# Evicting the queries of two attention branches one 512-wide unit at a time, branch by branch, where pairs of both branches were evicted together

## The chip, the cores and the metric

The kernel runs on one core of a Trainium2 chip. The metric is the device time of one execution in microseconds; the profile is one execution recorded by the hardware profiler, whose span runs from the first to the last instruction.

## The reference

Two linear-attention branches, A and B, read the same input x (2048 rows of 640) and are mixed by a gate. Each has its own weights. 32 heads of width 20; everything is bf16 outside the kernel.

```python
def branch(x, wqkv, wo):
    q, k, v = split_heads(x @ wqkv)                  # 32 heads of 20
    phi = lambda t: where(t > 0, t + 1, exp(t)) + 1e-6
    pq, pk = phi(q), phi(k)
    kv  = einsum("bhsd,bhse->bhde", pk, v)
    z   = sum_s(pk)
    num = einsum("bhqd,bhde->bhqe", pq, kv)
    den = einsum("bhqd,bhd->bhq", pq, z) + 1e-6
    return merge_heads(num / den) @ wo

g = sigmoid((x * gate_w).sum(-1))
out = g * branch(x, A...) + (1 - g) * branch(x, B...)
```

## The kernel before

The kernel never forms the values. It runs these stages:

1. **Keys** (`k_part`, `k_both`): per tile of 128 rows, x @ wk for A and B, and phi of it into `PK`. phi is three instructions: an exp on ScalarE from PSUM into the buffer `EK` (L560), a min-and-add on VectorE within `EK` (L564), and a max-and-add on VectorE from PSUM and `EK` into the result (L570). For most tiles a unit is 128 x 512.
2. **G** (`g_unit`): phi(k) transposed times x, five parts per branch, 16 tiles deep. Each is copied out and transposed by a DMA into `GT`. `gone["A"]` and `gone["B"]` name the last matmul of each branch's G.
3. **M** (`m_unit`): GT times wv gives the 32 small kv matrices, which VectorE masks (L651) into `MB`. **Weight products** (`wp_unit`): M times wo, six tiles per branch, copied to `WS`, stored to memory by `wp_store` (tensor `wrowsB` for B) and read back in another order by `wp_rows` into `WP` (WPA, WPB). So phi(q) @ WP is already num @ wo.
4. **Queries** (`q_pair`): the rows are cut into four blocks b of 512, the 640 columns into five parts k. One call does one (b, k) for both branches: ten matmuls of 512 columns, five for A into one PSUM bank and five for B into the bank beside it, then phi over 128 x 1024 at once (exp L753, min-and-add L755, max-and-add L759) into `FE`, whose halves `PQ` are the phi(q) of A and B. `FE` is shared with `PK`, so the queries may only begin when G has read the keys.
5. **Denominators** (`dens`) for two blocks at a time: phi(q) times `ZBD`, copied with the epsilon added into `DN` (L791). **Scaling** (`scale_q`) per block: reciprocal into `RC` (L802), a store of it to memory (`factor`), a load that spreads it over the partitions (`RX`), and multiplies in place over phi(q) of A and B (L820).
6. **Finals** (`final`): per tile of 128 rows, phi(q) @ WPA and phi(q) @ WPB, each two groups of 320 columns in a pair of banks; ScalarE scales A by its gate (L865), VectorE scales B and adds (L871), and SP stores the row tile.

All matmuls of a tile go through one helper, so they all carry L383; tell them by tile names: `ps<-XT,WQA` and `ps<-XT,WQB` are queries, `ps<-FE,ZBDA` and `ps<-FE,ZBDB` denominators, `ps<-WPA,FE` and `ps<-WPB,FE` finals. DMAs carry L372.

**Order.** Nothing runs in the order written by itself. Every operation is put into a planner (`_Sched`) with a duration from simple formulas and a latency of 180 or 190 ns to its readers. The planner simulates the engines: at each step it takes, for the engine that can start earliest, among the operations that could start within 20 ns of the earliest the one that was written first. So a call that is written earlier ranks higher. PSUM's eight banks and the rings of buffers (`EK`: six slots of 640, used by the queries before as three double slots) are given out in the same simulation. The result is a fixed order per engine; on the chip each engine runs its list in that order and waits by semaphores. A late operand therefore holds everything behind it on that engine.

The order in which the second half is written, before the change: block 0 of the queries, M of B, block 1, denominators of blocks 0 and 1, block 2, scaling of 0, block 3, scaling of 1, denominators of blocks 2 and 3, finals of block 0, scaling of 2, finals of 1, scaling of 3, finals of 2 and 3. The weight products of B are placed between the pairs of block 1 by `WPAT`, the last of them after the first pair of block 2, followed there by the store and the load of its rows.

Of the kernel before, what the change touches and what calls it, by code (L numbers as in the profile page):

```python
# [15 lines left out]
ACT = mybir.ActivationFunctionType  # L16
ALU = mybir.AluOpType

S = 2048
D = 640  # L20
# [4 lines left out]
NC = 5  # L25
EPS = 1e-6
HALF = 320
WPAT = ((1, 0), (1, 1), (1, 2), (1, 3), (1, 4), (2, 0))
XW = 672
PE_GHZ = 2.4  # L30

# [255 lines left out]
def _act_ns(n, psum=True):  # L287
    return n / 1.2 + (52.0 if psum else 94.0)


def _dve_ns(n, rate=1):
    return n / (0.96 * rate) + 68.0
# [6 lines left out]
def bass_gated_mix__linear_attn_block__linear_attn_block__prompt_kernel(nc, A_x, A_wqkv, A_wo, B_x, B_wqkv, B_wo, gate_w, out):  # L299
# [4 lines left out]
    XS = ("A", "B")  # L304

    with ExitStack() as es:
# [6 lines left out]
        XT = sb("XT", [128, NC, S])  # L313
        WQ = {X: sb("WQ" + X, [128, NC, D]) for X in XS}
# [4 lines left out]
        FE = sb("FE", [128, 2, NT * D])  # L319
        PKJ = FE[:, :, :].rearrange("p x (t f) -> p x t f", f=D)  # L320
        PK = {X: PKJ[:, x, :, :] for x, X in enumerate(XS)}
        PQ = {X: FE[:, x, :].rearrange("p (k s) -> p k s", s=S) for x, X in enumerate(XS)}
# [9 lines left out]
        NEK = 6  # L332
        EK = sb("EK", [128, NEK, D])
# [25 lines left out]
        def pair(t, n):  # L359
            b0, b1 = t.banks  # L360
            return PS[:, b0 : b1 + 1, 0:n]
# [15 lines left out]
        def mms(name, steps, reads, writes, cols, lat=190.0, par=1, prio=None, after=None):  # L377


            def fn(pe):  # L380
                ins = None
                for o, l, r, a, z, tp in steps():
                    ins = pe.matmul(o, l, r, start=a, stop=z, tile_position=tp, skip_group_check=True)  # L383
                return ins

            return sch.op("PE", fn, cols / PE_GHZ / par, reads=reads, writes=writes, name=name, lat=lat, prio=prio, after=after)
# [93 lines left out]
                    _dve_ns(128 * (c1 - c0)), reads=[(tt,)], writes=[("XTC", t, c) for c in range(c0, c1)], name="xev%d" % t,  # L480
                )

        ring = {"ek": _Ring(NEK), "eq": _Ring(NEK // 2), "dn": _Ring(2), "rx": _Ring(2), "os": _Ring(NOS), "ts": _Ring(NTS)}

        def phi_k(X, t, tile):
            es = _Tile(1, ring["ek"])
# [203 lines left out]
        def wp_store(X):  # L690
            dma(
                "SP", "ws" + X, WD[X].ap()[0:600, :].rearrange("(q p) f -> p q f", p=120), WS[:, 0:5, :], reads=[("WS", q) for q in range(5)],
                writes=[("WD", X, 0)], us=2.0,
            )
# [32 lines left out]
                "DVE", lambda e: e.reciprocal(GA[:, :, :], GE[:, :, :]), 330, reads=[("GE", 0), ("GE", 1)], writes=[("GA",)], name="ga",  # L727
            )

        def q_pair(b, k):  # L730

            tile = _Tile(2)
            es = _Tile(1, ring["eq"])

            def eq():
                return EK[:, :, :].rearrange("p n f -> p (n f)")[:, 1280 * es.slot : 1280 * es.slot + 1024]

            def eq2():
                return eq().rearrange("p (x s) -> p x s", x=2)

            dst = FE[:, :, S * k + 512 * b : S * k + 512 * b + 512]
            span = range(S * k + 512 * b, S * k + 512 * b + 512)
            over = [("F", X, w, t) for X in XS for w in ("k", "k5") for t in range(span[0] // D, span[-1] // D + 1)]

            def steps():
                return [
                    (PS[:, tile.banks[x], :], WQ[X][:, c, k : D : NC], XT[:, c, 512 * b : 512 * b + 512], c == 0, c == NC - 1, None)
                    for x, X in enumerate(XS) for c in range(NC)
                ]

            xt = [("XTC", t, c) for t in range(4 * b, 2) for c in range(NC)] + [("XT", t) for t in range(max(2, 4 * b), 4 * b + 4)]
            o = mms("q%d%d" % (b, k), steps, xt + [("WQ", X) for X in XS], [(tile,)], 2 * NC * 518, after=gone["B"])
            sch.op("ACT", lambda e: e.activation(eq2(), pair(tile, 512), ACT.Exp), _act_ns(1024), reads=[(tile,)], writes=[(es,)], name="eq%d%d" % (b, k))  # L753
            sch.op(
                "DVE", lambda e: e.tensor_scalar(eq(), eq(), 1.0, EPS, op0=ALU.min, op1=ALU.add), _dve_ns(1024, 4),  # L755
                reads=[(es,)], writes=[(es,)], name="tq%d%d" % (b, k),
            )
            sch.op(
                "DVE", lambda e: e.scalar_tensor_tensor(out=dst, in0=pair(tile, 512), scalar=0.0, in1=eq2(), op0=ALU.max, op1=ALU.add),  # L759
                _dve_ns(1024), reads=[(tile,), (es,)], writes=[("PQ", X, k, b) for X in XS] + over, name="sq%d%d" % (b, k),  # L760
            )
            return o

        def dens(b0):

            dtile = _Tile(1)

            def den():
                r = []
                for k in range(NC):  # L770
                    for x, X in enumerate(XS):
                        q = PQ[X][:, k, 512 * b0 : 512 * b0 + 1024].rearrange("p (b h f) -> p b h f", b=2, h=2)
                        for h in (0, 1):
                            g = 2 * x + h
                            r.append((
                                PS[32 * g : 32 * g + 32, dtile.banks[0], :].rearrange("p (b f) -> p b f", b=2), ZBD[X][:, k, :],
                                q[:, :, h, :], k == 0, k == NC - 1, (0, 32 * g),
                            ))
                return r

            mms(
                "den%d" % b0, den, [("ZBD", X) for X in XS] + [("PQ", X, k, b) for X in XS for k in range(NC) for b in (b0, b0 + 1)],
                [(dtile,)], 5 * 540,
            )
            ds = []
            for b in (b0, b0 + 1):
                d = _Tile(1, ring["dn"])
                ds.append(d)
                sch.op(
                    "ACT",  # L790
                    lambda e, d=d, lo=256 * (b - b0): e.activation(  # L791
                        DN[:, d.slot, :], PS[:, dtile.banks[0], lo : lo + 256], ACT.Identity, bias=EP[:, 0:1]
                    ),
                    _act_ns(256), reads=[(dtile,), ("EP",)], writes=[(d,)], name="dn%d" % b,
                )
            return ds

        def scale_q(b, ds, pieces):

            def rec(e):  # L800
                with nc.allow_low_precision(reason="the factor is a bf16 matmul operand"):
                    return e.reciprocal(RC[:, ds.slot, :], DN[:, ds.slot, :])  # L802

            sch.op("DVE", rec, 1740, reads=[(ds,)], writes=[(ds,)], name="rc%d" % b)
            rep = FD[b].ap()
            dma(
                "SP", "fw%d" % b, rep.rearrange("g h r f -> (g h) r f"), lambda: RC[:, ds.slot, :].unsqueeze(1).to_broadcast([128, 4, 256]),
                reads=[(ds,)], writes=[("FD", b)], us=0.6,
            )
            xs = _Tile(1, ring["rx"])  # L810
            dma(
                "SP", "fr%d" % b, lambda: RX[:, xs.slot, :].rearrange("p (g f) -> p g f", f=256), rep.rearrange("g h r f -> (h r) g f"),
                reads=[("FD", b)], writes=[(xs,)], us=0.6,
            )
            w = 512 // pieces
            for j in range(pieces):
                for x, X in enumerate(XS):
                    def fn(e, j=j, x=x, X=X):
                        v = PQ[X][:, :, 512 * b + w * j : 512 * b + w * j + w]
                        return e.tensor_tensor(  # L820
                            out=v, in0=v, in1=RX[:, xs.slot, 512 * x + w * j : 512 * x + w * j + w].unsqueeze(1).to_broadcast([128, NC, w]), op=ALU.mult
                        )
                    ts = range(4 * b + 4 * j // pieces, 4 * b + 4 * (j + 1) // pieces)
                    sch.op(
                        "DVE", fn, _dve_ns(NC * w, 2), reads=[(xs,)] + [("PQ", X, k, b) for k in range(NC)],
                        writes=[("PQS", X, t) for t in ts], name="ml%s%d" % (X, b),
                    )
# [98 lines left out]
        wp_store("A")  # L926
        zbd("B")
        def queries(b):
            for k in range(NC):
                q_pair(b, k)  # L930
                for i, p in enumerate(WPAT):
                    if p == (b, k):
                        wp_unit("B", (i - 1) % 6)
                        if i == 0:
                            wp_rows("A")
                        if i == 5:
                            wp_store("B")
                            wp_rows("B")

        def finals(b):  # L940
            for t in range(4 * b, 4 * b + 4):
# [5 lines left out]
        queries(0)  # L947
        m_unit("B")
        queries(1)
        d0, d1 = dens(0)  # L950
        queries(2)
        scale_q(0, d0, 2)
        queries(3)
        scale_q(1, d1, 2)
        d2, d3 = dens(2)
        finals(0)
        scale_q(2, d2, 2)
        finals(1)
        scale_q(3, d3, 4)
        finals(2)  # L960
        finals(3)

# [32 lines left out]
```

## Time and profile before

| | us |
|---|---|
| median of 3 runs | 192.31 (191.86 to 192.77) |
| profiled execution | 191.86 |
| its span | 190.5 |
| TensorE / VectorE / ScalarE busy in it | 185.6 / 125.7 / 73.0 |
| query stage on TensorE (first query to the last) | 94.96 to 143.3 |
| second denominator | from 148.95 |

TensorE is PE in the profile, VectorE DVE, ScalarE ACT, SyncE SP, whose queue issues most DMAs. Lines of the timelines give start, duration, engine, line, operation, result<-operands with shapes, a count where neighbours are merged, and in brackets the idle time of the engine before it with what ended that. Lines of the groups give busy time in all, mean ns of one instruction, and idle time before the group with what ended it. A line of the windows gives the stretch, its length, the busy time of PE, PEld (weight loads), DVE, ACT and POOL with their counts, the granted TensorE clock, the DMA share and GB/s. The granted clock was 1.00 in every stretch of the profile.

### The profile page before, as it was taken

How to read it: one execution, taken by the hardware profiler on the slowest of the kernel's cores; microseconds unless marked ns; L12 is line 12 of the kernel's file. 1: busy time of each engine (PE TensorE's matmuls, PEld its weight loads, DVE VectorE, ACT ScalarE, POOL GpSimd, SP SyncE). 2: the span in 40 equal slices, each digit the busy share in tenths (PEclk: the TensorE clock that was granted, in tenths of full speed). 3: DMA queues.
4: the chain of work that ended last, by engine and by line, in shares of the span. 5: the costliest groups of instructions: out<-in, count | busy, mean ns of one | idle time of the engine just before them, and what ended most of it. 6: DMA issues, size and time to landing. Idle time of an engine off the chain costs nothing.

```text
span 190.5 us, 3131 instructions
## 1 busy us (share of the span) xinstructions
PE 185.6 (97%) x1280; PEld 124.2 (65%) x1289; DVE 125.7 (66%) x235; ACT 73.0 (38%) x109; POOL 8.2 (4%) x14
## 2 busy tenths in 40 slices
PE   7999999999999999999999999999979999999995
PEld 2655555555888888888855655555536577777774
DVE  0399898989500019996157896679699977943324
ACT  2265556555211221113244366654443413331332
POOL 8900000000000000000000000000000000000000
DMA  6999699991011111113152023069400154311212
GB/s 192 286 225 198 194 390 364 342 235 31 0 38 34 34 34 38 34 34 38 34 126 70 3 58 137 9 156 271 121 0 0 69 153 140 107 53 50 72 69 69
DMA packets 31967, 21.48 MB, mean 113 GB/s; under 512 B 16850, under 2 KB 31698, under 8 KB 31954
## 3 DMA queue, kind: packets, MB, share of 16 engines
q1 hardware_dynamic: 31234, 20.48, 39.5%
q10 hardware_dynamic: 720, 0.82, 1.3%
q8 instruction: 10, 0.16, 0.4%
q14 instruction: 3, 0.02, 0.0%
HBM read 12.05 MB, written 5.31 MB: 91 GB/s over the span
## 4 chain that ended last, share of the span: by engine, by line
PE 88%; DMA 6%; DVE 4%; issue 1%; ACT 0%; DVEq 0%
PE ps L383 87%; DMA factor<-RC 3%; DMA XN<-in_A_x_dram 2%; DVE FE L820 2%; DMA RX<-factor 1%; DVE FE L759 1%; DVE RC L802 1%; PE ps L468 1%; DVE EK L755 0%; DVE OL L871 0%; ACT DN L791 0%; DVEq L276 0%
## 5 line engine op out<-in xcount | busy, mean ns | idle before, releaser
L383 PE MATMUL ps<-XN,FE 128*128 128x320 bf16 x320 | 44.3, 300 | 0.0
L383 PE MATMUL ps<-WK,XT 128*128 128x512 bf16 (+2 forms) x246 | 43.7, 337 | 0.2
L383 PEld LDWEIGHTS ps<-XN,FE 128*128 128x128 bf16 x320 | 37.5, 118 | 6.0
L383 PEld LDWEIGHTS ps<-WK,XT 128*128 128x128 bf16 x250 | 24.2, 98 | 19.2 <-issue 0.2
L753 ACT ACTIVATE EK<-ps 128x1024 bf16<-128x1024 f32 x20 | 20.5, 1023 | 24.0 <-PE ps L383 21.9
L560 ACT ACTIVATE EK<-ps 128x512 bf16<-128x512 f32 (+1 forms) x42 | 21.4, 526 | 16.2 <-PE ps L383 16.2
L383 PE MATMUL ps<-XT,WQA 128*128 128x512 bf16 x95 | 24.0, 379 | 1.6 <-DVE FE L759 1.0
L383 PE MATMUL ps<-XT,WQB 128*128 128x512 bf16 x100 | 24.8, 379 | 0.0
L759 DVE SCALAR_TENSOR_TENSOR FE<-ps,EK 128x1024 bf16<-128x1024 f32 x20 | 24.3, 1217 | 0.4
L383 PE MATMUL ps<-WPA,FE 128*128 128x320 bf16 (+1 forms) x165 | 24.5, 295 | 0.0
L383 PE MATMUL ps<-WPB,FE 128*128 128x320 bf16 (+1 forms) x165 | 24.5, 295 | 0.0
L570 DVE SCALAR_TENSOR_TENSOR FE<-ps,EK 128x512 bf16<-128x512 f32 (+1 forms) x42 | 23.9, 597 | 0.5
L865 ACT ACTIVATE TS<-ps,GA 128x640 f32<-128x640 f32 (+2 forms) x18 | 13.1, 734 | 27.5 <-PE ps L383 27.5
L871 DVE SCALAR_TENSOR_TENSOR OS<-ps,GA,TS 128x640 bf16<-128x640 f32 x15 | 13.0, 876 | 13.3 <-PE ps L383 13.3
L597 ACT ACTIVATE GS<-ps 128x640 bf16<-128x640 f32 x10 | 7.0, 703 | 36.8 <-PE ps L383 36.8
L383 PEld LDWEIGHTS ps<-WPA,FE 128*128 128x128 bf16 x165 | 15.9, 98 | 6.5 <-issue 0.4
L383 PEld LDWEIGHTS ps<-WPB,FE 128*128 128x128 bf16 x165 | 15.9, 98 | 5.8
L383 PEld LDWEIGHTS ps<-XT,WQB 128*128 128x128 bf16 x100 | 11.7, 117 | 9.8
L383 PEld LDWEIGHTS ps<-XT,WQA 128*128 128x128 bf16 x100 | 11.5, 118 | 10.0 <-DVE FE L759 1.5
L711 DVE SCALAR_TENSOR_TENSOR GP<-XN,GWB 128x640 bf16<-128x640 bf16 x16 | 13.3, 828 | 4.1 <-PE ps L383 3.6
L820 DVE TENSOR_TENSOR FE<-FE,RX 128x1280 bf16<-128x1280 bf16 (+1 forms) x20 | 12.7, 688 | 3.4 <-DMA RX<-factor 3.4
L564 DVE TENSOR_SCALAR EK<-EK 128x512 bf16<-128x512 bf16 (+1 forms) x42 | 11.3, 271 | 3.0
(52 smaller groups left out, 78.7 us busy)
## 6 DMA issues: line engine op xcount, KB each, us to landing
out_dram<-OS SPq DMA_DIRECT2D x15, 160.0 KB, 1.8
XN<-in_A_x_dram SPq DMA_DIRECT2D x3, 640.0 KB, 8.1
factor<-RC SPq DMA_DIRECT2D x4, 256.0 KB, 3.2
RX<-factor SPq DMA_DIRECT2D x4, 256.0 KB, 3.0
WVA<-in_A_wqkv_dram SPq DMA_DIRECT2D x1, 800.0 KB, 10.6
WQA<-in_A_wqkv_dram SPq DMA_DIRECT2D x1, 800.0 KB, 11.9
WVB<-in_B_wqkv_dram SPq DMA_DIRECT2D x1, 800.0 KB, 11.3
WQB<-in_B_wqkv_dram SPq DMA_DIRECT2D x1, 800.0 KB, 12.1
```

What stands on the lines that cost most here:

```text
L383: ins = pe.matmul(o, l, r, start=a, stop=z, tile_position=tp, skip_group_check=True)
L468: ins = pe.transpose(PSB[:, tt.banks[0], 128 * c : 128 * c + 128], XN[:, t, 128 * c : 128 * c + 128], IDN[:, :])
L560: "ACT", lambda e, ps=ps, ek=ek: e.activation(ek(), ps(), ACT.Exp), _act_ns(n), reads=[(tile,)], writes=[(es,)],
L564: "DVE", lambda e, ek=ek: e.tensor_scalar(ek(), ek(), 1.0, EPS, op0=ALU.min, op1=ALU.add), _dve_ns(n, 4),
L570: return e.scalar_tensor_tensor(out=out, in0=two(ps()), scalar=0.0, in1=two(ek()), op0=ALU.max, op1=ALU.add)
L597: "ACT", lambda e: e.activation(GS[:, k, :].rearrange("p (h f) -> p h f", f=HALF), pair(tile, HALF), ACT.Copy),
L711: lambda e, t=t: e.scalar_tensor_tensor(out=GP[:, :], in0=XN[:, t, 0:D], scalar=1.0, in1=GWB[:, :], op0=ALU.mult, op1=ALU.mult, accum_out= ...
L753: sch.op("ACT", lambda e: e.activation(eq2(), pair(tile, 512), ACT.Exp), _act_ns(1024), reads=[(tile,)], writes=[(es,)], name="eq%d%d" % ( ...
L759: "DVE", lambda e: e.scalar_tensor_tensor(out=dst, in0=pair(tile, 512), scalar=0.0, in1=eq2(), op0=ALU.max, op1=ALU.add),
L820: return e.tensor_tensor(out=v, in0=v, in1=RX[:, xs.slot, 512 * x + w * j : 512 * x + w * j + w].unsqueeze(1).to_broadcast([128, NC, w]), ...
L865: "ACT", lambda e: e.activation(t_ap(), acc(), ACT.Copy, scale=GA[:, 0, t : t + 1]), _act_ns(hi - lo),
L871: lambda e: e.scalar_tensor_tensor(out=o_ap(), in0=acc(), scalar=GA[:, 1, t : t + 1], in1=t_ap(), op0=ALU.mult, op1=ALU.add),
```

## The change

`q_pair` is replaced by `q_unit`, which does one (b, k) of one branch: five matmuls into one bank, and phi over 128 x 512. There are 40 such units where there were 20 pairs. Further:

- a block is written as its five units of A and then its five units of B, where it was five pairs;
- units of A wait for `gone["A"]`, those of B for `gone["B"]`; the pairs waited for `gone["B"]`;
- the exp result lies in a slot of the ring `EK` with its six slots; the ring of three double slots is gone;
- the weight products of B come two units behind in block 1 (`WPLAG`): after A2, A3, A4, B0, B1 and B2, the last tile number 4 after B2; the store and load of B's rows are written after block 1, and the load of A's rows after A2 of block 1;
- `dens` no longer makes the copies into `DN`; each `scale_q` makes its own;
- the scaling of block 0 is written before block 2, not after it.

```diff
-WPAT = ((1, 0), (1, 1), (1, 2), (1, 3), (1, 4), (2, 0))
+WPLAG = 2
...
-        ring = {"ek": _Ring(NEK), "eq": _Ring(NEK // 2), "dn": _Ring(2), "rx": _Ring(2), "os": _Ring(NOS), "ts": _Ring(NTS)}
+        ring = {"ek": _Ring(NEK), "dn": _Ring(2), "rx": _Ring(2), "os": _Ring(NOS), "ts": _Ring(NTS)}
...
-        def q_pair(b, k):
-
-            tile = _Tile(2)
-            es = _Tile(1, ring["eq"])
...
+        def q_unit(X, b, k):
+            tile = _Tile(1)
+            es = _Tile(1, ring["ek"])
+
+            def ek():
+                return EK[:, es.slot, 0:512]
+
+            dst = PQ[X][:, k, 512 * b : 512 * b + 512]
...
             def steps():
                 return [
-                    (PS[:, tile.banks[x], :], WQ[X][:, c, k : D : NC], XT[:, c, 512 * b : 512 * b + 512], c == 0, c == NC - 1, None)
-                    for x, X in enumerate(XS) for c in range(NC)
+                    (PS[:, tile.banks[0], :], WQ[X][:, c, k : D : NC], XT[:, c, 512 * b : 512 * b + 512], c == 0, c == NC - 1, None)
+                    for c in range(NC)
                 ]
...
-            ds = []
-            for b in (b0, b0 + 1):
-                d = _Tile(1, ring["dn"])
-                ds.append(d)
-                sch.op(
-                    "ACT",
-                    lambda e, d=d, lo=256 * (b - b0): e.activation(
-                        DN[:, d.slot, :], PS[:, dtile.banks[0], lo : lo + 256], ACT.Identity, bias=EP[:, 0:1]
-                    ),
-                    _act_ns(256), reads=[(dtile,), ("EP",)], writes=[(d,)], name="dn%d" % b,
-                )
-            return ds
-
-        def scale_q(b, ds, pieces):
+            return dtile
+
+        def scale_q(b, dtile, pieces):
+
+            ds = _Tile(1, ring["dn"])
+            lo = 256 * (b % 2)
+            sch.op(
+                "ACT",
+                lambda e: e.activation(DN[:, ds.slot, :], PS[:, dtile.banks[0], lo : lo + 256], ACT.Identity, bias=EP[:, 0:1]), _act_ns(256),
+                reads=[(dtile,), ("EP",)], writes=[(ds,)], name="dn%d" % b,
+            )
...
         def queries(b):
-            for k in range(NC):
-                q_pair(b, k)
-                for i, p in enumerate(WPAT):
-                    if p == (b, k):
-                        wp_unit("B", (i - 1) % 6)
-                        if i == 0:
+            for X in XS:
+                for k in range(NC):
+                    q_unit(X, b, k)
+                    q = 5 * (X == "B") + k - WPLAG
+                    if b == 1 and 0 <= q < 6:
+                        wp_unit("B", (q - 1) % 6)
+                        if q == 0:
                             wp_rows("A")
-                        if i == 5:
-                            wp_store("B")
-                            wp_rows("B")
...
         queries(1)
-        d0, d1 = dens(0)
+        wp_store("B")
+        wp_rows("B")
+        d01 = dens(0)
+        scale_q(0, d01, 2)
         queries(2)
-        scale_q(0, d0, 2)
         queries(3)
-        scale_q(1, d1, 2)
-        d2, d3 = dens(2)
+        scale_q(1, d01, 2)
+        d23 = dens(2)
         finals(0)
-        scale_q(2, d2, 2)
+        scale_q(2, d23, 2)
         finals(1)
-        scale_q(3, d3, 4)
+        scale_q(3, d23, 4)
```

More of the change, by code (lines that the diff above doesn't have):

```diff
@@ L728, in gates @@
             )
-        def q_pair(b, k):
-            tile = _Tile(2)
-            es = _Tile(1, ring["eq"])
[L735 to L741, printed above, removed]
+        def q_unit(X, b, k):
[4 more added lines that the diff above has]
+            dst = PQ[X][:, k, 512 * b : 512 * b + 512]
@@ L742, in q_pair @@
             span = range(S * k + 512 * b, S * k + 512 * b + 512)
-            over = [("F", X, w, t) for X in XS for w in ("k", "k5") for t in range(span[0] // D, span[-1] // D + 1)]
+            over = [("F", X, w, t) for w in ("k", "k5") for t in range(span[0] // D, span[-1] // D + 1)]
             def steps():
                 return [
-                    (PS[:, tile.banks[x], :], WQ[X][:, c, k : D : NC], XT[:, c, 512 * b : 512 * b + 512], c == 0, c == NC - 1, None)
-                    for x, X in enumerate(XS) for c in range(NC)
-                ]
@@ L751, in q_pair @@
-            xt = [("XTC", t, c) for t in range(4 * b, 2) for c in range(NC)] + [("XT", t) for t in range(max(2, 4 * b), 4 * b + 4)]
-            o = mms("q%d%d" % (b, k), steps, xt + [("WQ", X) for X in XS], [(tile,)], 2 * NC * 518, after=gone["B"])
-            sch.op("ACT", lambda e: e.activation(eq2(), pair(tile, 512), ACT.Exp), _act_ns(1024), reads=[(tile,)], writes=[(es,)], name="eq%d%d" % (b, k))
+                    (PS[:, tile.banks[0], :], WQ[X][:, c, k : D : NC], XT[:, c, 512 * b : 512 * b + 512], c == 0, c == NC - 1, None)
@@ L754, in q_pair @@
+                    for c in range(NC)
+                ]
+            mms("q%s%d%d" % (X, b, k), steps, [("XTC", t, c) for t in range(4 * b, 2) for c in range(NC)] + [("XT", t) for t in range(max(2, 4 * b), 4 * b + 4)] + [("WQ", X)], [(tile,)], NC * 518, after=gone[X])
             sch.op(
-                "DVE", lambda e: e.tensor_scalar(eq(), eq(), 1.0, EPS, op0=ALU.min, op1=ALU.add), _dve_ns(1024, 4),
-                reads=[(es,)], writes=[(es,)], name="tq%d%d" % (b, k),
+                "ACT", lambda e: e.activation(ek(), PS[:, tile.banks[0], :], ACT.Exp), _act_ns(512), reads=[(tile,)],
+                writes=[(es,)], name="eq%s%d%d" % (X, b, k),
@@ L757, in q_pair @@
             )
             sch.op(
-                "DVE", lambda e: e.scalar_tensor_tensor(out=dst, in0=pair(tile, 512), scalar=0.0, in1=eq2(), op0=ALU.max, op1=ALU.add),
-                _dve_ns(1024), reads=[(tile,), (es,)], writes=[("PQ", X, k, b) for X in XS] + over, name="sq%d%d" % (b, k),
-            )
-            return o
+                "DVE", lambda e: e.tensor_scalar(ek(), ek(), 1.0, EPS, op0=ALU.min, op1=ALU.add), _dve_ns(512, 4),
+                reads=[(es,)], writes=[(es,)], name="tq%s%d%d" % (X, b, k),
+            )
@@ L764, in dens @@
+            sch.op(
+                "DVE",
+                lambda e: e.scalar_tensor_tensor(
+                    out=dst, in0=PS[:, tile.banks[0], :], scalar=0.0, in1=ek(), op0=ALU.max, op1=ALU.add
+                ),
+                _dve_ns(512), reads=[(tile,), (es,)], writes=[("PQ", X, k, b)] + over, name="sq%s%d%d" % (X, b, k),
+            )
         def dens(b0):
@@ L784, in dens @@
             )
-            ds = []
-            for b in (b0, b0 + 1):
-                d = _Tile(1, ring["dn"])
-                ds.append(d)
-                sch.op(
-                    "ACT",
-                    lambda e, d=d, lo=256 * (b - b0): e.activation(
-                        DN[:, d.slot, :], PS[:, dtile.banks[0], lo : lo + 256], ACT.Identity, bias=EP[:, 0:1]
-                    ),
-                    _act_ns(256), reads=[(dtile,), ("EP",)], writes=[(d,)], name="dn%d" % b,
-                )
-            return ds
-        def scale_q(b, ds, pieces):
+            return dtile
+        def scale_q(b, dtile, pieces):
+            ds = _Tile(1, ring["dn"])
+            lo = 256 * (b % 2)
+            sch.op(
+                "ACT",
+                lambda e: e.activation(DN[:, ds.slot, :], PS[:, dtile.banks[0], lo : lo + 256], ACT.Identity, bias=EP[:, 0:1]), _act_ns(256),
+                reads=[(dtile,), ("EP",)], writes=[(ds,)], name="dn%d" % b,
+            )
             def rec(e):
```

## The prediction

> **What bounds the kernel now.** I read the page first, then the groups kept apart by shape, then the timelines around the one place where TensorE stands still, and last the chain of waits.
>
> ```profile
> span 190.5 us, 3131 instructions
> PE 185.6 (97%) x1280; PEld 124.2 (65%) x1289; DVE 125.7 (66%) x235; ACT 73.0 (38%) x109; POOL 8.2 (4%) x14
> PE   7999999999999999999999999999979999999995
> DVE  0399898989500019996157896679699977943324
> PE 88%; DMA 6%; DVE 4%; issue 1%; ACT 0%; DVEq 0%
> ```
>
> TensorE is the bound: 185.6 of 190.5 us. The whole budget for a gain is the 4.9 us in which it is idle, and most of that is the start and the tail, which the change does not touch. The one lower digit inside (7, the 30th slice, 138 to 143 us) lies in the query stage. The timelines of VectorE, TensorE and the SP queue show it:
>
> ```profile
> 133.34 1.23 DVE L759 SCALAR_TENSOR_TENSOR FE<-ps,EK 128x1024 bf16<-128x1024 f32 x1
> 136.22 3.04 DVE L820 TENSOR_TENSOR FE<-FE,RX 128x1280 bf16<-128x1280 bf16 x4 [1.66 <-DMA RX<-factor]
> 139.17 0.76 DVE L755 TENSOR_SCALAR EK<-EK 128x1024 bf16<-128x1024 bf16 x2
> 141.12 1.27 PE L383 MATMUL ps<-XT,WQA 128*128 128x512 bf16 x5 [1.05 <-DVE FE L759]
> 148.95 0.39 PE L383 MATMUL ps<-FE,ZBDA 128*32 128x512 bf16 x2
> 122.89 0.34 SPq L372 DMA_DIRECT2D wrowsB<-WS  x1
> 127.88 0.35 SPq L372 DMA_DIRECT2D WPB<-wrowsB  x1
> 128.28 2.57 SPq L372 DMA_DIRECT2D factor<-RC  x2
> 133.42 1.12 SPq L372 DMA_DIRECT2D RX<-factor  x2
> ```
>
> VectorE waits 1.66 us for the factors of query block 0, multiplies for 3 us, and the query pairs behind it keep their PSUM banks so long that the last pair of block 3 starts 1.05 us late. The factors were late because their store stood in the SP queue behind WPB (issued 127.88, factor 128.28, though the reciprocal ended at 127.15) and shared the DMA engines with its 800 KB: 5.1 us to land, against a median of 3.2. From 148.95 on TensorE never waits again until the tail.
>
> The prices, by shape:
>
> ```profile
> L759 DVE SCALAR_TENSOR_TENSOR FE<-ps,EK 128x1024 bf16<-128x1024 f32 x20 | 24.3, 1217 | 0.4
> L753 ACT ACTIVATE EK<-ps 128x1024 bf16<-128x1024 f32 x20 | 20.5, 1023 | 24.0 <-PE ps L383 21.9 <-DVE FE L759 2.1
> L755 DVE TENSOR_SCALAR EK<-EK 128x1024 bf16<-128x1024 bf16 x20 | 8.4, 424 | 7.2 <-ACT EK L753 7.2
> L570 DVE SCALAR_TENSOR_TENSOR FE<-ps,EK 128x512 bf16<-128x512 f32 x28 | 19.3, 688 | 0.5
> L560 ACT ACTIVATE EK<-ps 128x512 bf16<-128x512 f32 x28 | 16.7, 597 | 16.2 <-PE ps L383 16.2
> L564 DVE TENSOR_SCALAR EK<-EK 128x512 bf16<-128x512 bf16 x28 | 8.2, 294 | 2.4
> ```
>
> The key stage already runs the three instructions of the changed kernel in their exact shapes, so nothing has to be guessed from afar. Its timeline shows how they follow one another, and the windows how full VectorE already is at the end of the query stage:
>
> ```profile
> 30.15 0.56 DVE L564 TENSOR_SCALAR EK<-EK 128x512 bf16<-128x512 bf16 x2
> 30.62 1.02 DVE L570 SCALAR_TENSOR_TENSOR FE<-ps,EK 128x512 bf16<-128x512 f32 x2
> 140.00:150.00 10.00, 8.91 (x71) 5.52 (x70) 10.00 (x13) 3.63 (x4) 0.00 (x0) 1.00 0.01 2
> ```
>
> **Part by part. TensorE.** The same 200 query matmuls, 216 ns each (five start 1.08 us after the five before). Reordering them costs nothing: weights change at every matmul in both forms.
>
> **Splitting the evictions.** Two halves for one whole: 2 x 688 - 1217 = 159 ns and 2 x 294 - 424 = 164 ns on VectorE, 2 x 597 - 1023 = 171 ns on ScalarE. Times 20: 6.5 us more VectorE work (125.7 to 132.2), 3.4 us more on ScalarE. ScalarE has 1.08 us for a unit of 0.60, plus 0.70 for each of six weight tiles that TensorE also spends 0.27 us on; it stays hidden (uncovered, 3.4 us). VectorE needs 0.98 us for a unit by whole durations, 0.82 where neighbours overlap (the x2 at 30.62, a 512 and a 256, took 1.02 together and 0.688 + 0.415 = 1.10 apart, so 0.08 each). Against TensorE's 1.08 both fit, but the slack shrinks from 2.16 - 1.64 = 0.52 per pair to 0.20 to 0.52 per two units. That is the cover, and where it is gone the 6.5 us is the price.
>
> [...]
>
> **Smaller tiles.** A unit holds one bank instead of two and one 512-wide slot of six instead of a double slot of three: the same buffer depth, in finer grains. No gain or loss by itself.
>
> **Waiting for one branch only.** Units of A now wait for G of A, not of B. The plan before has TensorE without a gap there (48.74 to 94.96), so none can move forward: 0.
>
> **Weight products of B and their stores.** Six tiles of 0.27 us, now all within query block 1. The last now follows B2 of block 1. Block 0 takes TensorE from 94.96 to 105.76 and M of B to 106.94; eight units and six tiles later it is 106.94 + 8 x 1.08 + 6 x 0.27 = 117.2, the copy ends 1.2 later (0.2, 0.3 behind an exp, 0.7) at 118.4, so the store is issued 4.5 us earlier (118.4 for 122.89), and WPB at about 123.3 for 127.88. On SP both then stand ahead of the factors, whose store no longer waits for WPB's issue. The read of WPA's rows moves back by less than a pair, to about 111 to 113 us, and is needed by the finals after 142: 0.
>
> **The denominator.** It needs the last unit of block 1; TensorE ends that at 106.94 + 10.8 + 1.62 = 119.36, and its eviction takes 0.2 to the exp (96.90 to 97.10 in the first pair), 0.60, 0.04, 0.29, 0.04, 0.69: 1.86 more, 121.2. Two units of block 2 (2.16) fill the gap instead of two pairs, so it starts at 121.6, not 123.58, and the next unit 1.44 later, at 123.04 (as 123.58 to 125.02). Mask work of M (2 x 1.03 + 2 x 0.28 = 2.6 us on VectorE) delays the first units by 1.3 us; ten units with at least 0.10 each and six tiles of 0.27 give back 2.6, so that debt is gone.
>
> **Reciprocal and scaling of block 0.** The copy DN ends 1.8 us after the denominator's start (123.58 to 125.37 before): 123.4; reciprocal to 125.1 (0.08 of its 1.75 overlaps). The second copy DN and the second reciprocal now rank behind block 3. ScalarE is idle there, so the copy stays where it was; the reciprocal goes into the 180 ns that the planner assumes between an add and its max, as before (the planner's costs, 479, 201 and 601 ns for a unit, 1079 on TensorE, only tell the order here). The multiplies of block 0 now rank ahead of block 2; the planner has their factors due after four more units, A3 to B1: VectorE ends the second reciprocal at 127.0, then A2's max (0.6) and four units (3.3): 130.9. Factors: store issued 125.2 while WPB (issued 123.3, about 4.7) is still moving; the store landed 0.8 us after WPB in the trace (133.40, and 127.88 + 4.7 = 132.6), so about 128.8 (128.4 by its median of 3.2), and RX 2.8 later: 131.2 to 131.6. So VectorE waits 0.3 to 0.7 us, not 1.66, and has multiplied by about 134.4 (136.22 to 139.2 before). Eight units of TensorE lie beyond the first waiting one (B2, started 128.4): its bank is needed at 137.1 and free at about 135.7. The 1.05 us stall is gone, with 1.4 us to spare.
>
> **The new wait.** The second denominator needs all of block 3. TensorE ends the queries at 123.04 + 18 x 1.08 = 142.5 and fills with finals (1.36 us a half). By the planner's own costs the denominator falls after three halves: 146.6, with 1.0 us planned slack. VectorE: 134.4 + 12 x 0.82 + a last unit with one multiply wedged in (0.25 + 0.74 + 0.69) = 145.9; by 0.94 a unit (no overlap of add and max) 147.4. So no wait, or 0.8 us. What stands behind it on TensorE is every final.
>
> **Sum.** Before, 148.95 follows two whole finals; after, 146.6 follows one and a half, and 1.36 is still to come: 190.5 - 148.95 + 1.36 = 42.9 remain. Span 146.6 + 42.9 = 189.5, 1.0 less; up to 147.4 + 42.9 = 190.3. I take 189.6, 0.9 less. The profiled execution took 191.86, 1.36 outside the span; the median of the runs is 192.31, so 191.4.
>
> **Rivals.** *VectorE becomes the bound from the scaling on (slower).* Its place is the second denominator; it decides as soon as that starts after 190.5 - 42.9 = 147.6. Price: with whole durations, 134.7 + 13 x 0.98 and all four multiplies ahead of the last unit (4 x 0.74) give 150.4, span 193.3, 195.1 as a time; with factors as late as before (136.22), 139.2 + 9.84 + 1.68 = 150.7, the same. For it: VectorE stands at 10.00 of 10 between 140 and 150 us already, and SP or WPB may be late. Against: the key stage runs these shapes at 2.6 us per 2.70 without holding TensorE. Halfway it is 193.6.
>
> *The stall only moves (no change).* The denominator waits 0.5 to 1.5 us; span 190.0 to 191.0, time 191.8 to 192.8. For it: a start at 146.6 against 145.9 is a thin margin.
>
> *It does nothing early.* That A may start before G of B is through has no room, as said; the time would then rest on the two cases above alone, 191.4 to 192.8.
>
> **How the numbers follow.** Forecast 0.45 (190.9 to 191.7, so 0.25 of it faster and 0.20 within), the stall that moves or no effect 0.25, VectorE as the bound 0.30. About 0.5%, 0.96 us, is what a measurement of this kernel can tell from no change. Faster 0.25, same 0.45, slower 0.30. The range runs from 190.8 (the 1.05 and the small 0.2 us gaps at q32 and the denominator all gone) to 194.3, past the middle of the slow case; the likeliest case alone is 190.9 to 191.7.
>
> **What would show it.** Right: no TensorE wait of 1 us near 140; the denominator at about 121.6; the store of WPB's rows near 118.4; the wait for RX under 1 us; VectorE busy 132 us, ScalarE 76; a second denominator near 146.6 that waits for nothing. Wrong: TensorE waiting on an eviction of VectorE before the second denominator, VectorE full from 125 to 150, multiplies of block 1 ahead of the last units, or the factor's store still 5 us.

## The result and the profile after

| | before | after |
|---|---|---|
| median, first comparison (6 runs each) | 192.88 | 190.69 |
| ratio, first comparison | | 0.989 (0.9851 to 0.9929) |
| median, second comparison (27 and 12 runs) | 192.09 | 190.95 |
| ratio, second comparison | | 0.9945 (0.9919 to 0.9971) |
| profiled execution / its span | 191.86 / 190.5 | 190.71 / 189.4 |
| first matmul of G to the end of VectorE's last operation, in the trace | 48.74 to 188.87: 140.13 | 48.95 to 187.73: 138.78 |

The changed kernel is faster by 0.6 to 1.1%. The last row is the sharpest measure: what lies ahead of G (the loads and the keys) is untouched and scatters, with G beginning between 48.47 and 49.75 us in the fourteen profiles of this study, while from G on two profiles of one kernel agree within 0.13 us. On that measure the change is worth 1.35 us, 0.7%.

The page of the changed kernel:

```profile
span 189.4 us, 3199 instructions
PE 185.6 (98%) x1280; PEld 123.9 (65%) x1289; DVE 130.0 (69%) x275; ACT 76.4 (40%) x129; POOL 8.2 (4%) x14
PE   8999999999999999999999999999999999999995
DVE  0398988998600009996179998898999959933324
PE 94%; DMA 3%; SPq 1%; issue 1%; DVE 0%; DVEq 0%
```

TensorE does the same 185.6 us of work, the dip in the 30th slice is gone, and in the chain that ended last it has 94% for 88%: the 4% of VectorE and the factor DMAs are out of it (the 3% of DMA that stay are loads of the key weights `WK` at the start). VectorE is busier by 4.3 us, ScalarE by 3.4.

The timelines of SP, VectorE and TensorE, at the places shown of before:

```profile
118.36 0.33 SPq L372 DMA_DIRECT2D wrowsB<-WS  x1
123.35 0.35 SPq L372 DMA_DIRECT2D WPB<-wrowsB  x1
125.23 2.31 SPq L372 DMA_DIRECT2D factor<-RC  x2
128.59 1.38 SPq L372 DMA_DIRECT2D RX<-factor  x2
```

```profile
131.49 3.03 DVE L817 TENSOR_TENSOR FE<-FE,RX 128x1280 bf16<-128x1280 bf16 x4 [0.74 <-DMA RX<-factor]
144.97 0.68 DVE L758 SCALAR_TENSOR_TENSOR FE<-ps,EK 128x512 bf16<-128x512 f32 x1
```

```profile
136.89 5.56 PE L383 MATMUL ps<-XT,WQB 128*128 128x512 bf16 x25
142.28 1.52 PE L383 MATMUL ps<-WPA,FE 128*128 128x320 bf16 x10
146.45 0.39 PE L383 MATMUL ps<-FE,ZBDA 128*32 128x512 bf16 x2
```

B's rows are stored 4.5 us earlier, so WPB is issued 1.9 us ahead of the factors and lands at 127.80: their store takes 3.3 us to land (issued 125.23, landed 128.58), not 5.1. It still lands 0.78 us behind WPB, as before (133.40 behind 132.61); what changed is that WPB itself comes sooner. VectorE waits 0.74 us for RX, not 1.66, and queries, three halves of finals and the second denominator follow one another on TensorE with no wait: 25 matmuls from 136.89 end in a start at 142.28, 5.39 us, 25 x 0.216. The last eviction ends at 145.65, 0.8 us before the denominator starts.

### The profile page after: what moved, and what is told of

Same layout as the page of the kernel before. It is cut to its first block, busy times and chain, and to the rows that moved or that the text cites. A ratio compares the mean times of both kernels' runs of the same rounds, so it can differ in the third digit from the quotient of the medians.

```text
span 189.4 us, 3199 instructions
## 1 busy us (share of the span) xinstructions
PE 185.6 (98%) x1280; PEld 123.9 (65%) x1289; DVE 130.0 (69%) x275; ACT 76.4 (40%) x129; POOL 8.2 (4%) x14
## 4 chain that ended last, share of the span: by engine, by line
PE 94%; DMA 3%; SPq 1%; issue 1%; DVE 0%; DVEq 0%
PE ps L383 94%; DMA WK<-in_B_wqkv_dram 3%; SPq L372 1%; DVE OL L868 0%; DVEq L276 0%
## 5 line engine op out<-in xcount | busy, mean ns | idle before, releaser
L749 ACT ACTIVATE EK<-ps 128x512 bf16<-128x512 f32 x40 | 23.9, 597 | 18.5 <-PE ps L383 15.6
L758 DVE SCALAR_TENSOR_TENSOR FE<-ps,EK 128x512 bf16<-128x512 f32 x40 | 26.7, 684 | 0.7
L383 PE MATMUL ps<-XT,WQB 128*128 128x512 bf16 x99 | 22.5, 379 | 0.1
L383 PE MATMUL ps<-XT,WQA 128*128 128x512 bf16 x96 | 22.2, 379 | 0.3 <-DVE EK L753 0.2
```

Source lines behind the costliest of these rows:

```text
L749: "ACT", lambda e: e.activation(ek(), PS[:, tile.banks[0], :], ACT.Exp), _act_ns(512), reads=[(tile,)],
L758: lambda e: e.scalar_tensor_tensor(out=dst, in0=PS[:, tile.banks[0], :], scalar=0.0, in1=ek(), op0=ALU.max, op1=ALU.add),
```

## The experiments

All times "from G" are from the first matmul of G to the end of VectorE's last operation (the last columns of the output) in a profile: 140.13 before, 138.78 after. Theory: the gain comes from the factors of block 0 no longer being held up by the 800 KB read of B's rows. Rivals: the finer units bring it, the rank of the scaling brings it, or the profiled execution of before was not a usual one.

**The kernel before, again** (no edit).

> The kernel before with nothing changed, profiled and timed against itself. If the medians differ by the drift between sessions alone, the ratio is 1.000 within 0.4%, and a second profile shows the start (first query at 94.96 in the first profile) moved by some tenths of a us while the wait of TensorE for VectorE near 140 us stays at 1.0 us (0.9 to 1.2). If the first profile was a lucky execution, with a shorter stall than most (its time of 191.86 us was the lowest of six), this one shows a stall of 1.5 to 2 us, because the factor store lands later than 5.1 us after its issue.

Ratio 1.001 (0.9987 to 1.0033). From G 140.26. G began 0.34 us later than in the first profile, and the same query pair waited a little longer:

```profile
141.60 1.27 PE L384 MATMUL ps<-XT,WQA 128*128 128x512 bf16 x5 [1.18 <-DVE FE L760]
```

The factor store again took 5.05 us. The first profile was a usual one but for its early start; the stall belongs to the kernel.

**The kernel after, again** (no edit).

> The changed kernel with nothing further changed, for more runs beside the kernel before. In the profiles the span from the first query to the end is 95.5 and 95.7 us before and 94.2 after; the start ahead of the first query scatters between 94.96 and 95.98 us in kernels that do the same there. If that is all, the ratio is 0.9925 (0.991 to 0.994), 1.4 us, and the 0.989 of the first comparison lay at the edge of its interval. If the changed kernel has a further gain that one profile does not show, the ratio stays at 0.990 or below.

Ratio 0.9945 (0.9919 to 0.9971), from G 138.78 (48.77 to 187.55). The first ratio of 0.989 does not repeat in its middle; the two intervals share 0.9919 to 0.9929, and the traces say 0.993.

**Pairs, the rows of B read behind the factors.**

```diff
-  "SP", "wp" + X, ..., reads=[("WD", X, 0), ("WD", X, 5)],
+  "SP", "wp" + X, ..., reads=[("WD", X, 0), ("WD", X, 5)] + [("FD", 0)] * (X == "B"),
...
   scale_q(0, d0, 2)
+  wp_rows("B")
   queries(3)
```

(and `wp_rows("B")` taken out of `queries`)

> Pairs and every order as before, but the read of B's rows (WPB) is written after the scaling of block 0 and waits for the store of its factors; nothing else moves. It undoes the one thing that the forecast blamed for the late factors. Theory: the store is issued at the end of the reciprocal (about 127.2) and lands in 2.6 to 3.2 us, RX is there by 133.2, before VectorE asks for it (134.6); no wait of TensorE near 140, and from the first query to the end it takes 94.2 to 94.5 us instead of 95.5 to 95.7; ratio 0.993 to 0.995. Rival (pairs stall there anyway, since a bank pair is only free when both halves are out): a wait of at least 0.5 us stays, ratio above 0.997.

Ratio 0.9933 (0.9909 to 0.9957), from G 138.78 (48.47 to 187.25). SP and TensorE:

```profile
126.92 0.61 SPq L372 DMA_DIRECT2D factor<-RC  x1
129.56 0.39 SPq L372 DMA_DIRECT2D RX<-factor  x1
130.05 0.45 SPq L372 DMA_DIRECT2D WPB<-wrowsB  x1
```

```profile
139.65 1.24 PE L383 MATMUL ps<-XT,WQA 128*128 128x512 bf16 x5
```

The store lands in 2.6 us, and the pair that stood still before starts 1.08 us after the one ahead of it (138.57). One DMA moved, pairs kept, and the whole gain of the change is there. One thing else moved with it: the planner put one of the four multiplies ahead of a max-and-add that it had followed. That delays this eviction by 0.74 us and leaves VectorE's work up to the evictions behind it the same, so it is not what brings the gain. The theory holds: the late read of B's rows made the stall, and without it the pairs are as fast as the changed kernel.

**Pairs, the weight products packed earlier.**

```diff
-WPAT = ((1, 0), (1, 1), (1, 2), (1, 3), (1, 4), (2, 0))
+WPAT = ((1, 0), (1, 1), (1, 1), (1, 2), (1, 2), (1, 3))
```

> Pairs as before, with the weight products of B packed into the first four pairs of block 1, so that the store and the read of B's rows are issued some 4 us earlier; nothing else. Theory (the gain is the factors coming sooner because WPB is out of their way): WPB issued about 123.5, factor store issued at the end of the reciprocal (about 127.2) and landed in 2.6 to 3.2 us, RX about 133.2, no wait of TensorE near 140: 1.0 to 1.3 us off the span, ratio 0.993 to 0.995. Rival (the split into units brings the gain, by finer release of banks): the stall keeps at least 0.6 us and the ratio is above 0.997.

Ratio 0.9983 (0.9962 to 1.0004), from G 139.62: 0.5 us gained, not 1.0 to 1.3. The stall near 140 went (no wait there), but the packing made another: a pair of block 1 waited 0.65 us for VectorE (0.81 from start to start), and the chain that ended last runs to it through the masks of M (L651) and one max-and-add. VectorE itself was no later: that max-and-add starts 62.7 us after G's first matmul in either kernel. But two weight tiles now stand ahead of the pair where one stood. Each holds two banks, as a pair does, so two pairs and two tiles held all eight, and the pair had to wait until the first of those pairs was evicted, behind the masks (its max-and-add ran from 112.41 to 113.64, the waiting pair starts at 113.69).

**Pairs, the scaling ranked ahead of block 2.**

```diff
-        queries(2)
         scale_q(0, d0, 2)
+        queries(2)
```

> Pairs as before, with the scaling of block 0 written ahead of block 2; nothing else. The planner then gives the same order up to the multiplies, which go one pair earlier or stay where they were. Theory: same as before, stall of 1.0 us (0.8 to 1.6, longer if the multiplies wait with more pairs behind them), ratio 0.998 to 1.003. Rival (the rank of the scaling brings the gain): stall under 0.3 us, ratio 0.995.

Ratio 1.0001 (0.9977 to 1.0024), from G 140.15, wait 1.07 us. The rank alone is worth nothing.

**Pairs, both edits.**

> Pairs as before with both edits: B's rows stored early and the scaling of block 0 ranked ahead of block 2. Theory (order alone carries the change, the split is neutral): no stall near 140, the second denominator after two whole finals at about 147.7, span 189.2 with a start as in the profile of before, ratio 0.989 to 0.995, and level with the changed kernel within 0.3%. Rival (units matter): at least 0.6 us slower than the changed kernel, ratio above 0.996.

Ratio 0.9985 (0.9959 to 1.0011), from G 139.67, with the same new wait in block 1 (0.66). It missed its forecast for the reason given under the packing, and does not speak for the units.

**The changed kernel, the scaling ranked behind block 2 again.**

> The changed kernel with the scaling of block 0 written behind block 2 again. Its multiplies then rank behind block 2, and the planner puts them some two units later, one of them between an add and its max. If the rank brought nothing, the time is that of the changed kernel within 0.2% (94.1 to 94.4 us from the first query to the end, ratio to before 0.9925). If the rank matters, the second denominator is late by 0.5 us or more, or TensorE waits near 140.

Ratio 0.9946 (0.992 to 0.9972), from G 138.78. That part of the change is worth nothing here either.

**The split alone**: `q_unit` in the kernel before, called for A and then B of one part; all else as written before.

> The split alone: units in place of pairs, with the weight products, the copies DN and the scaling written where they were before, and A and B of one part still side by side. If finer units by themselves bring the gain (denominator after two units, so the factor store gets ahead of WPB on SP, and the multiplies come before the queue is long): denominator at about 121.3 to 121.6, factor store issued ahead of WPB, no wait near 140, 94.2 to 94.5 us from the first query to the end, ratio 0.992 to 0.994. If the gain needs the early store of B's rows: a wait of 0.5 us or more near 140 or at the second denominator, 94.9 us or more, ratio 0.996 to 1.000.

Ratio 1.007 (1.004 to 1.0101), from G 140.76. It is slower than both kernels. SP, VectorE and TensorE:

```profile
124.33 0.34 SPq L372 DMA_DIRECT2D wrowsB<-WS  x1
125.50 2.51 SPq L372 DMA_DIRECT2D factor<-RC  x2
129.81 0.35 SPq L372 DMA_DIRECT2D WPB<-wrowsB  x1
130.53 1.13 SPq L372 DMA_DIRECT2D RX<-factor  x2
```

```profile
135.73 0.83 DVE L824 TENSOR_TENSOR FE<-FE,RX 128x1280 bf16<-128x1280 bf16 x1 [2.51 <-DMA RX<-factor]
```

```profile
148.98 0.39 PE L383 MATMUL ps<-FE,ZBDA 128*32 128x512 bf16 x2 [1.63 <-DVE FE L758]
```

The denominator did come 2.4 us sooner (counted from G), and with it the factor store, which now met the other row transfer: 5.0 us beside the 750 KB store, then 5.2 us for RX beside WPB. VectorE waited 2.51 us, and the second denominator 1.63.

**The changed kernel, the rows of B late again**: a weight tile after every second unit, the last one in block 2, the store and read behind it.

```diff
-                    if b == 1 and 0 <= q < 6:
+                    q = q if b == 1 else 10 + q if b == 2 else -1
+                    if 0 <= q < 12 and q % 2 == 0:
+                        q //= 2
...
+                        if q == 5:
+                            wp_store("B")
+                            wp_rows("B")
```

> The changed kernel with one thing undone: the weight products of B come after every second unit instead of every unit, so the last of them falls into block 2 and the rows of B are stored some 5 us later, together with the factors. Theory (the early store carries the gain): the factor store is issued at about 125.4 as before but moves beside the 750 KB of rows, lands after 5 us, and RX beside the 800 KB of WPB, another 5: RX at about 135.7, VectorE waits 2 to 3 us, the second denominator waits 1 to 2 us for VectorE; from the start of G to the last output 140.5 to 141.0 us as in the split alone (140.76), against 138.78 for the changed kernel; ratio 1.003 to 1.008. Rival (writing block by block A before B is what separates the changed kernel from the split alone): 138.8 to 139.3, ratio under 0.997.

Ratio 1.0035 (1.0014 to 1.0056); from G 141.26, 2.5 us lost against the changed kernel, a little more than expected. The factor store took 5.8 us and RX 5.3. The wait fell elsewhere than expected, on the first two halves of the finals, which waited for max-and-adds of the last units, and none was left for the denominator (that these units held the banks which the halves need is read from the kernel, not from the trace):

```profile
143.99 1.52 PE L383 MATMUL ps<-WPA,FE 128*128 128x320 bf16 x10 [0.93 <-DVE FE L758]
146.59 1.52 PE L383 MATMUL ps<-WPB,FE 128*128 128x320 bf16 x10 [1.08 <-DVE FE L758]
```

**The split alone, the rows of B stored behind the factors**: as the split alone, with the store waiting for `("FD", 0)` and written, with the read, behind the scaling of block 0.

> The split alone, with the store of B's rows made to wait for the factor store of block 0 and so its read behind it; the order of all else stays that of the split alone. Theory (the split costs nothing once no row traffic meets the factors): factor store landed in 2.6 to 3.2 us, RX at about 131, no wait of TensorE; 138.8 to 139.0 us from the start of G to the last output, ratio 0.993. Rival (the split by its 6.5 us of VectorE work is what made the split alone slow): still a wait of 0.7 us or more at the second denominator, 139.5 us or more, ratio above 0.997.

Ratio 0.9916 (0.9894 to 0.9939), from G 138.79 (48.79 to 187.58). The factor store took 2.6 us; no wait. So the split costs nothing where the factors come in time. Since the pairs reach the same time by the same means, the split brings nothing either.

**1.6 us more VectorE work behind the multiplies of block 0**, in the changed kernel and in the pairs with the rows read late.

```diff
+            for _ in range(2 * (b == 0)):
+                sch.op("DVE", lambda e: e.scalar_tensor_tensor(out=GP[:, :], in0=XN[:, 0, 0:D], scalar=1.0, in1=GWB[:, :], ...), ...)
```

> The changed kernel with two idle products of 128 x 640 on VectorE (0.83 us each, 1.5 to 1.6 together) behind the multiplies of block 0; their result is read by nobody. It measures how much more VectorE work the changed kernel bears before the second denominator. By its trace the last eviction ends at 145.65 and the denominator starts at 146.45, so 0.8 us are free, and one multiply of 0.73 can move behind it: expected 138.8 to 139.2 us from the start of G to the last output, a wait of 0 to 0.3 us. If VectorE is the hidden bound, the whole 1.6 us shows: 140.4.

> The same two idle products in the kernel with pairs whose read of B's rows is behind the factors. Its last eviction ends 0.68 us ahead of the second denominator, and pairs hold four double banks, so a unit of TensorE must find two free at once. If finer units release banks better, pairs show more of the 1.6 us: a wait of 0.5 to 1.0 us near 137 to 140 or at the denominator, 139.3 to 139.8 us. If the grain does not matter: 138.8 to 139.2, as with units.

Units: from G 139.69, 0.91 lost. Pairs: 139.27, 0.49 lost. TensorE of the two:

```profile
143.12 1.52 PE L383 MATMUL ps<-WPA,FE 128*128 128x320 bf16 x10 [0.30 <-DVE FE L758]
```

```profile
141.34 1.27 PE L383 MATMUL ps<-XT,WQA 128*128 128x512 bf16 x5 [0.30 <-DVE FE L759]
```

The expectations had it the other way round: units bear less, not more. With units the largest wait came at the first final, before the denominator could matter. Why is not shown: units and pairs differ in how they hold banks, but the units also carry more VectorE work and another order, and each figure is one profile.

## Why the prediction was right in its steps and wrong in its time

**Right, step by step.** Forecast and measured: rows stored 118.4 / 118.36; WPB 123.3 / 123.35; denominator 121.6 / 121.63; reciprocal done 125.1 / 125.12; factor store issued 125.2 / 125.23; multiplies from 131.2 to 131.6 / 131.49, done 134.4 / 134.43; last eviction 145.9 / 145.65; second denominator 146.6 / 146.45, with no wait for VectorE; span 189.5 / 189.4. The named cause was confirmed by one moved DMA, and neither VectorE as the bound nor the moved stall occurred. But part of this agreement is luck. The forecast counts from the profile of before, in which G begins at 48.74, and in the profile after it begins at 48.95. On a common start every measured time is 0.22 us earlier: the second denominator comes at 146.23 for 146.6, and the span is 189.19 for 189.5. The gain is then 1.35 us where the sum had 1.0.

**The step that failed: the size of the gain, in TensorE's path to the second denominator.** The sum added up TensorE's work from 106.94 (block 1), gave the first denominator 1.44 us up to the next unit, and came to 146.6. Both numbers were read from groups whose first matmul is missing from the trace. The page of before has 100 weight loads (PEld) for the queries of A and 95 matmuls, and one of the groups that is short stands behind the denominator:

```profile
L383 PEld LDWEIGHTS ps<-XT,WQA 128*128 128x128 bf16 x100 | 11.5, 118 | 10.0 <-DVE FE L759 1.5
L383 PE MATMUL ps<-XT,WQA 128*128 128x512 bf16 x95 | 24.0, 379 | 1.6 <-DVE FE L759 1.0
125.02 1.03 PE L383 MATMUL ps<-XT,WQA 128*128 128x512 bf16 x4 [0.18 <-issue]
```

It shows four matmuls for five weight loads (from 124.77), so the first began about one matmul, 0.216 us, ahead of 125.02. The group at 106.94 is the same (weight loads from 106.69). Where the record is there, in the profile after, the next unit follows the denominator (121.63) by 1.20 us:

```profile
122.83 3.43 PE L383 MATMUL ps<-XT,WQA 128*128 128x512 bf16 x14
```

On the common start the first denominator came 0.19 us sooner than the sum had it and the next unit another 0.24; the three halves of finals, up to the denominator, took 4.17 and not 4.1. That is 0.19 + 0.24 - 0.07 = 0.36 us by which the second denominator came sooner than the sum had it, and the gain is so much larger.

**Where the 1.35 us lie in the traces.** The 1.05 us of the stall was read from the idle column. The starts tell more:

```profile
138.83 1.24 PE L383 MATMUL ps<-XT,WQB 128*128 128x512 bf16 x5
```

The next group starts at 141.12, 2.29 us later, where starts are otherwise 1.08 apart: 1.21 us are lost (1.35 in the second profile). The groups are drawn 1.24 long but start every 1.08, so 0.16 of every wait hides under the drawn end of the group ahead. Another 0.03 is that the group that had waited took 1.11 to the next start, not 1.08. And 0.11 was a wait of the second denominator: by starts it was due at 148.75 and came at 148.95 before (the last eviction ended at 148.80), at 146.36 and 146.45 after. 1.21 + 0.03 + 0.11 = 1.35. The mechanism was right, and its size was short.

**The lower end of the range.** Its 190.8 is the 192.31 of before less the 1.05 and two "small 0.2 us gaps at q32 and the denominator", some 1.45 in all. That is about the size of the gain, but partly by luck: the stall was larger than the 1.05, and the gap at q32 was no gap. TensorE in the profile of before:

```profile
135.81 1.03 PE L383 MATMUL ps<-XT,WQA 128*128 128x512 bf16 x4
```

The next group starts at 136.68, 0.87 us on, four matmuls and not five: here too the first record is missing, and the "gap" of 0.21 is one matmul of 0.216.

**The base.** The time was formed on a median of three runs, 192.31, and the range had no room for scatter on its fast side. The median of all six runs of that comparison is 192.88; later medians of the kernel before are 192.51, 192.09 and 192.46. Taking 1.35 to 1.48 from the later three (1.48 is the second profile of before, 140.26, against 138.78) gives 190.6 to 191.2; the measured medians, 190.69 and 190.95, lie there, the first 0.1 below the range, the second inside it. With 1.35 in it the time would have been put at 191.0. That the first comparison showed more, 2.2 us, is left to the scatter of single runs (between the lowest and the highest of one kernel in one comparison lie 1.4 to 2.6 us); no run here shows another cause, and none proves this one.

**VectorE's extra work.** Forecast 6.5 us, and 4.3 busy (130.0 for 125.7). By shape:

```profile
L758 DVE SCALAR_TENSOR_TENSOR FE<-ps,EK 128x512 bf16<-128x512 f32 x40 | 26.7, 684 | 0.7
L753 DVE TENSOR_SCALAR EK<-EK 128x512 bf16<-128x512 bf16 x40 | 10.8, 286 | 2.3 <-ACT EK L749 1.5
```

By the durations of single instructions the extra is 6.0 us (684 and 286 ns, a little under the 688 and 294 that the forecast took). 26.7 + 10.8 against 24.3 + 8.4 is 4.8: most of the rest is overlap, which busy time counts once (two max-and-adds in a row took 1.28, not 1.37). Where units follow one another two by two, the two take 1.60 us, 0.80 each, within the 0.82 that the sum used. The extra work was there and did not decide, since it lay beside TensorE's work. The loss of slack that the prediction named agrees with 0.91 against 0.49 us lost under the same added work, though one profile of each is all there is.

**The chances.** VectorE as the bound had 0.30. It is a true danger one edit away: the split without the early rows lost 0.7%, with 1.63 us at the second denominator. What it turned on, SP and WPB, was followed in the prediction's own steps, which left 1.4 us to spare, and no unit waited; so the 0.30 was high by its own sum. The 0.45 for no change rested on the gain that was sized too small.

## What to carry to other kernels

Follow a stall back past the engine that holds it to the transfer it waits for, and past that to what shares the queue with it: here one 800 KB read that nobody needed for another 12 us (landed 132.6, first used 144.67) cost the whole 0.7%, and moving it alone gave as much as the whole rewrite. Size a wait on TensorE from start to start of equal groups and not from the idle column, and count the records of a group, against its weight loads, before a small gap is believed. Time a change that turns on tenths of a us from a point behind the part that scatters.

## What the runs showed of the hardware that was not expected

- A 256 KB store of factors, issued from SP, took 2.5 to 2.9 us to land with no large transfer moving ahead of it, or one about to land; 3.1 to 3.5 when it was issued 1.8 to 1.9 us behind the 800 KB read of WPB; and 5.0 to 5.8 when it was issued within 1.2 us of that read or of the 750 KB store of the rows. (A second store behind such a one took 3.7 to 4.0, in one profile 5.2.) The 256 KB load of RX took 2.6 to 3.4, and 5.2 to 5.3 behind a large transfer. In four profiles the first factor store was issued 2.6 to 5.0 us before a large transfer ahead of it landed, and it landed 0.77 to 0.79 us after that one, whichever direction that had: 133.40 after 132.61 (before), 128.58 after 127.80 (changed), 130.52 after 129.75 (split alone), 131.71 after 130.93 (rows late again). What makes them land in that order is not shown.
- The part ahead of G, the same in all kernels here, scatters by 1.28 us over fourteen profiles, and is the greatest part of what differs between the profiles of one kernel.
